# Softmax of attention tiles: exponentials head by head on ACT with a bias, in place of a subtraction and a sum on VectorE

## Chip, cores and metric

One core of one Trainium2 chip. The metric is the time of one execution in microseconds; the engines are named as in the profile: PE (TensorE matmul), PEld (its weight load), DVE (VectorE), ACT (ScalarE), POOL (GpSimd), SP (SyncE, which issues most DMAs).

## What is computed

Three layers in a row, all fp32: attention within chunks of 64 positions (8 batches, 8 heads, 576 positions, head size 64), a gated two-matrix layer (512 to 2048 to 512) on all 4608 tokens, and a layer of eight experts (512 to 1024 to 512) of which each token takes the best one, if its skip score is positive.

```python
scores = scale * np.matmul(q_c, k_c.transpose(0, 1, 2, 4, 3))
scores = scores - np.max(scores, axis=-1, keepdims=True)
attn = np.exp(scores)
attn = attn / (np.sum(attn, axis=-1, keepdims=True) + 1e-09)
out = np.matmul(attn, v_c)
...
h = x @ w_in
g = h * (1.0 / (1.0 + np.exp(-1.702 * h)))
return (g @ w_out).astype(np.float32)
```

## The kernel before, in words

The attention works on 36 tiles of 128 positions, all 8 heads of a tile at once. A tile goes through these steps (class `Att`): `a` transposes q and k on PE (line 141) and copies them out of PSUM on ACT (143); `b_mm` makes the scores with 32 small matmuls of 64x64 into two PSUM banks, one for even and one for odd heads (158); `b_post` is the softmax up to the exponential (160 to 173); `c0` on DVE sums, adds 1e-9, takes the reciprocal and multiplies (175 to 182); `c1` transposes the probabilities on PE (187) and copies them out on ACT (189); `d_mm` multiplies with v, again in 64x64 matmuls (207), and `d_post` copies the result out into `x1` (212). On PE one 64x64 matmul of the program stands as two records in the trace.

Four tiles come first, before any of the second layer can start. While they run, and during the first block behind them, the second layer's weights are converted from 64-bit floats, in 32 halves: ACT (`r`, 255; `lf`, 256), DVE (262, 263), POOL (264), ACT (`whi`, 276), DVE (`wlo`, 277). The function `tick` sets how they are interleaved.

The second layer then runs over nine blocks of 512 tokens. A block starts with `split_x1`, which splits its input into two parts, `xh` on ACT (285) and `xl` on DVE (286), and has 16 rounds. A round is 12 matmuls 128x512 into `hps` (`emit_h`, 296), a `tanh` on ACT (299), a product on DVE (300), a cast on ACT (`gh`, 306), a difference on DVE (`gl`, 307) and 12 matmuls into `yps` (`emit_y`, 316 to 320). The other 32 attention tiles are spread over the first eight blocks, five in the first and four or fewer in each of the others. In the round of a `burst` PE makes the value matmuls of the tile before and the scores of the next one into the same two banks (`sv`); the two banks of that tag (`at`) also take the transposes and the small routing matmuls. DVE does the gates of the third layer (353) between. The experts' layer follows behind the ninth block.

The engines each work through their queue in order. What order that is, a scheduler decides when the program is built: it plays the program's instructions through a model and places each where it finds it ready. The source therefore sets the dependencies and a preference, and a change of one engine's work can change the order of all engines.

## Time and profile before

| | us |
|---|---|
| median of 3 runs | 1224.9 (1224.62 to 1226.09) |
| the profiled execution | 1227.84 |
| its span in the trace | 1226.1 |
| PE busy | 1182.7 (96%) |
| DVE busy | 783.9 (64%) |
| ACT busy | 490.2 (40%) |
| POOL busy | 144.6 (12%) |

The span is the time from the first to the last record. Busy time is the sum of the time in which an engine had an instruction running; PE's matmuls are pipelined, so a busy PE need not be at its peak. The rows further down say which line, engine and tile they belong to; "L173" is line 173 of the kernel.

### The profile page before, as it was taken

What the parts mean: (1) busy time and instruction counts of PE and PEld (TensorE: products, weight loads), DVE (VectorE), ACT (ScalarE), POOL (GpSimd) and SP (SyncE); (2) the same over time, 40 slices, a digit from 0 to 9 for tenths busy, and PEclk for the clock granted to TensorE, in tenths of its full rate; (3) what the DMA queues carried; (4) which work ended last, traced back from release to release, by engine and by line L of the source; (5) the groups of instructions that cost most, each with busy time, mean ns of one, the idle gap of its engine ahead of it and who ended that gap; (6) DMA issues with size and microseconds to landing.
All of it is one profiled execution on the core that took longest, in us unless ns stands there. A gap on an engine that the chain in (4) does not pass through costs nothing. (4 is left out here: it accounts for less than half of the span.)

```text
span 1226.1 us, 20893 instructions
## 1 busy us (share of the span) xinstructions
PE 1182.7 (96%) x7984; PEld 991.8 (81%) x7984; DVE 783.9 (64%) x1771; ACT 490.2 (40%) x825; POOL 144.6 (12%) x137
## 2 busy tenths in 40 slices
PE   6798999999999999999999999999999999999995
PEld 4576788888888888888888888888788989999885
DVE  5889578369349548647736935943985686665531
ACT  5867443343332333324334333332344454444320
POOL 2344000010010010000001001001021023231110
PEclk9999999999999999999999999999999999999998
DMA  9756331131122113113113113202344677666540
GB/s 211 208 175 178 112 102 27 44 104 26 27 68 78 28 31 107 32 31 95 35 36 104 26 28 92 55 10 69 130 139 131 215 170 265 215 228 227 195 144 8
DMA packets 181848, 129.00 MB, mean 105 GB/s; under 512 B 122336, under 2 KB 155360, under 8 KB 181617
## 3 DMA queue, kind: packets, MB, share of 16 engines
q1 hardware_dynamic: 177072, 117.09, 33.4%
q0 software_dynamic: 4672, 10.54, 2.5%
q8 instruction: 64, 1.05, 0.4%
q14 instruction: 40, 0.32, 0.1%
HBM read 103.59 MB, written 25.04 MB: 105 GB/s over the span
## 5 line engine op out<-in xcount | busy, mean ns | idle before, releaser
L316 PE MATMUL yps<-whi,gh 128*128 128x512 f32 x576 | 228.7, 397 | 6.4 <-ACT gh L306 6.4
L296 PE MATMUL hps<-xh,whi 128*128 128x512 f32 x576 | 231.6, 405 | 3.2 <-DVE sg L300 3.2
L296 PE MATMUL hps<-xl,whi 128*128 128x512 f32 x576 | 227.5, 395 | 0.0
L296 PE MATMUL hps<-xh,wlo 128*128 128x512 f32 x576 | 227.0, 394 | 0.0
L317 PE MATMUL yps<-wlo,gh 128*128 128x512 f32 x576 | 225.6, 392 | 0.0
L300 DVE SCALAR_TENSOR_TENSOR sg<-sg,hps 128x512 f32<-128x512 f32 x144 | 98.3, 684 | 172.1 <-ACT sg L299 171.1
L353 DVE CUSTOM_DVE_ANT_0 junk<-x,wg 128x512 f32<-128x512 f32 x256 | 175.8, 687 | 4.0
L543 DVE TENSOR_TENSOR elo<-rawe,ehi 128x1024 fp32r<-128x1024 f32 x88 | 107.6, 1224 | 84.6 <-ACT ehi L542 84.5
L320 PE MATMUL yps<-whi,gl 128*128 128x512 f32 x576 | 156.0, 393 | 0.0
L299 ACT ACTIVATE sg<-hps 128x512 f32<-128x512 f32 x144 | 85.8, 598 | 163.4 <-PE hps L296 163.2
L542 ACT CAST ehi<-rawe 128x1024 fp32r<-128x1024 f32 x88 | 92.3, 1049 | 139.6 <-PE h2p L608 69.4
L306 ACT ACTIVATE gh<-sg 128x512 fp32r<-128x512 f32 x144 | 91.0, 632 | 118.3 <-DVE sg L300 104.8
L316 PEld LDWEIGHTS yps<-whi,gh 128*128 128x128 f32 x576 | 108.3, 188 | 30.9 <-ACT gh L306 7.8
L296 PEld LDWEIGHTS hps<-xh,whi 128*128 128x128 f32 x576 | 108.5, 190 | 26.3 <-DVE sg L300 4.1
L296 PEld LDWEIGHTS hps<-xh,wlo 128*128 128x128 f32 x576 | 108.9, 189 | 22.6
L320 PEld LDWEIGHTS yps<-whi,gl 128*128 128x128 f32 x576 | 108.0, 189 | 22.6 <-DVE gl L307 0.3
L317 PEld LDWEIGHTS yps<-wlo,gh 128*128 128x128 f32 x576 | 108.5, 188 | 21.8
L296 PEld LDWEIGHTS hps<-xl,whi 128*128 128x128 f32 x576 | 109.2, 190 | 20.6
L307 DVE SCALAR_TENSOR_TENSOR gl<-sg,gh 128x512 fp32r<-128x512 f32 x144 | 99.0, 688 | 33.4 <-ACT gh L306 21.7
L406 POOL DMA_INDIRECT tab<-pr,pos x36 | 37.8, 1049 | 682.3 <-DVE st L166 335.0
L608 PE MATMUL h2p<-xT,ehi 128*128 128x256 f32 x640 | 117.2, 283 | 0.0
L608 PEld LDWEIGHTS h2p<-xT,ehi 128*128 128x128 f32 x640 | 101.9, 191 | 2.6
(172 smaller groups left out, 1520.5 us busy)
## 6 DMA issues: line engine op xcount, KB each, us to landing
rawe<-in_moe_w_dram SPq DMA_DIRECT2D x88, 512.0 KB, 4.0
v<-in_v_dram SPq DMA_DIRECT2D x144, 64.0 KB, 2.7
x2d<-x SPq DMA_DIRECT2D x36, 256.0 KB, 3.1
out_dram<-x SPq DMA_DIRECT2D x36, 256.0 KB, 3.8
q<-in_q_dram SPq DMA_DIRECT2D x32, 256.0 KB, 3.7
k<-in_k_dram SPq DMA_DIRECT2D x32, 256.0 KB, 3.7
raw<-in_moe_w_in_dram SPq DMA_DIRECT2D x16, 512.0 KB, 4.0
raw<-in_moe_w_out_dram SPq DMA_DIRECT2D x16, 512.0 KB, 3.3
```

The source lines that it names most:

```text
L296: PE.matmul(ps, a, b[:, kk], start=(n == 0), stop=(n == 3 * KD - 1))
L299: ACT.activation(out=sg, in_=ps, func=AF.Tanh, scale=0.851)
L300: DVE.scalar_tensor_tensor(sg, sg, 1.0, ps, op0=ALU.add, op1=ALU.mult)
L306: ACT.activation(out=gh, in_=sg, func=AF.Copy, scale=0.5)
L307: DVE.scalar_tensor_tensor(gl, sg, 0.5, gh.bitcast(F32), op0=ALU.mult, op1=ALU.subtract)
L316: PE.matmul(ys[t], gh[:, cs], wh, start=first, stop=False)
L317: PE.matmul(ys[t], gh[:, cs], wl, start=False, stop=False)
L320: PE.matmul(ys[t], gl[:, cs], wh, start=False, stop=last)
L353: DVE.tensor_tensor_reduce(junk, xs[t], wg[:, e, :] if e < NE else ws, 1.0, 0.0, ALU.mult, ALU.add, lg[:, t, e:e + 1])
L542: ACT.copy(out=hi, in_=raw)
L543: DVE.tensor_tensor(lo, raw, hi.bitcast(F32), op=ALU.subtract)
L608: PE.matmul(ps[:, f], a[:, c], self.xT[:, b, kk], start=(m == 0), stop=(m == 3 * KD - 1))
```

## The change

The maxima go into a tile `nm`, which is multiplied by minus the softmax scale. ACT then makes the exponentials of each of the eight heads by itself, 64 numbers a row, straight from the scores in PSUM, with the head's negative scaled maximum as bias, and adds up each head's sum into `st`. The two subtractions, the exponential over all heads and the sum on DVE are gone. From here on the changed kernel's lines are one less than before's (ACT's `tanh` is L298 in place of L299, the value matmuls L206 in place of L207).

```diff
         def b_post(self, ps):
 
             self.p = self.T[0].rearrange("p j (g k) -> p j g k", g=2)
-            pw = self.p.rearrange("p (x h) g k -> p h g x k", h=2)
             self.st = ap.tile([P, NHP, 2], F32, tag="st", name="st", bufs=2)
+            sc = float(D) ** -0.5
+            nm = ap.tile([P, 2, NHP], F32, tag="nm", name="nm", bufs=2)
             for h2 in range(2):
-                DVE.tensor_reduce(self.st[:, :, h2], ps[h2], axis=AX.X, op=ALU.max)
-            for h2 in range(2):
-                DVE.tensor_tensor(
-                    pw[:, h2], ps[h2].rearrange("p (g x) k -> p g x k", g=2),
-                    self.st[:, :, h2:h2 + 1].rearrange("p (g x) o -> p g x o", g=2).to_broadcast(
-                        [P, 2, 2, CH]), op=ALU.subtract,
-                )
-            ACT.activation(out=self.p, in_=self.p, func=AF.Exp, scale=float(D) ** -0.5)
+                DVE.tensor_reduce(nm[:, h2], ps[h2], axis=AX.X, op=ALU.max)
+            DVE.tensor_scalar(nm, nm, -sc, None, op0=ALU.mult)
+            for hp in range(NHP):
+                for h2 in range(2):
+                    g, j = divmod(2 * hp + h2, NHP)
+                    ACT.activation(out=self.p[:, j, g], in_=ps[h2][:, hp], func=AF.Exp, scale=sc,
+                                   bias=nm[:, h2, hp:hp + 1], accum_out=self.st[:, j, g:g + 1])
 
         def c0(self):
-            DVE.tensor_reduce(self.st, self.p, axis=AX.X, op=ALU.add)
             DVE.tensor_scalar(self.st, self.st, 1e-9, None, op0=ALU.add)
             DVE.reciprocal(out=self.st, in_=self.st)
```

The scheduler places things anew, on all engines. Three places follow, of the kernel before and of the changed one apart; the tiles are the out and in of a row, and "x4" counts equal neighbours.

On DVE, the start of the program, from the maxima of the first tile on. Before:

```order
L166 TENSOR_REDUCE st<-s_170 128x4
L166 TENSOR_REDUCE st<-s_171 128x4
L168 TENSOR_TENSOR bA<-s_170,st 128x2x2x64
L168 TENSOR_TENSOR bA<-s_171,st 128x2x2x64
L262 TENSOR_SCALAR r<-r 128x512
L263 SCALAR_TENSOR_TENSOR a<-raw_110,r 128x512
L176 TENSOR_REDUCE st<-bA 128x8
```

Now:

```order
L167 TENSOR_REDUCE nm<-s_170 128x4
L167 TENSOR_REDUCE nm<-s_171 128x4
L168 TENSOR_SCALAR nm<-nm 128x8
L176 TENSOR_SCALAR st<-st 128x8
L177 RECIPROCAL st<-st 128x8
L178 TENSOR_TENSOR bA<-bA,st 128x512
L261 TENSOR_SCALAR r<-r 128x512
L262 SCALAR_TENSOR_TENSOR a<-raw_110,r 128x512
```

The first weight conversion (`r`, `a`) stood ahead of the first tile's sum and normalization, and now stands behind the normalization, which needs all eight exponentials.

On ACT, a burst in the middle of the program, from the `tanh` ahead of it on. Before:

```order
L299 ACTIVATE sg<-hps 128x512
L306 ACTIVATE gh<-sg 128x512
L212 COPY x_3691<-sv_4241 128x2x128
L173 ACTIVATE qT<-qT 128x512
L212 COPY x_3692<-sv_4242 128x2x128
L299 ACTIVATE sg<-hps 128x512
```

Now:

```order
L298 ACTIVATE sg<-hps 128x512
L305 ACTIVATE gh<-sg 128x512
L172 ACTIVATE qT,st<-sv_4877,nm 128x64
L172 ACTIVATE qT,st<-sv_4878,nm 128x64
L172 ACTIVATE qT,st<-sv_4877,nm 128x64
L172 ACTIVATE qT,st<-sv_4878,nm 128x64
L172 ACTIVATE qT,st<-sv_4877,nm 128x64
L172 ACTIVATE qT,st<-sv_4878,nm 128x64
L172 ACTIVATE qT,st<-sv_4877,nm 128x64
L172 ACTIVATE qT,st<-sv_4878,nm 128x64
L211 COPY x_4786<-sv_4877 128x2x128
L211 COPY x_4787<-sv_4878 128x2x128
```

One row between the two copies became eight rows ahead of both; the next `tanh` stands behind them.

On PE, the 64x64 matmuls of a burst (line 206 or 207: values; 158: scores) in the same stage. Before, a whole burst ends:

```order
L158 MATMUL sv_4751<-kT,qT 64x64
L158 MATMUL sv_4752<-kT,qT 64x64
L158 MATMUL sv_4751<-kT,qT 64x64
L158 MATMUL sv_4752<-kT,qT 64x64
L296 MATMUL hps<-xh,whi 128x512
L296 MATMUL hps<-xl,whi 128x512
```

Now, in one burst, the change from values to scores:

```order
L206 MATMUL sv_4877<-qT,v 64x64
L206 MATMUL sv_4878<-qT,v 64x64
L158 MATMUL sv_4877<-kT,qT 64x64
L315 MATMUL yps<-whi,gh 128x512
L316 MATMUL yps<-wlo,gh 128x512
L319 MATMUL yps<-whi,gl 128x512
L158 MATMUL sv_4878<-kT,qT 64x64
L158 MATMUL sv_4877<-kT,qT 64x64
```

And in another, the first value matmul alone:

```order
L295 MATMUL hps<-xl,whi 128x512
L295 MATMUL hps<-xh,wlo 128x512
L206 MATMUL sv_5350<-qT,v 64x64
L315 MATMUL yps<-whi,gh 128x512
L316 MATMUL yps<-wlo,gh 128x512
```

The 16 value and 16 score matmuls of a burst stood in one stretch in most bursts; in the changed kernel large matmuls stand between them in some bursts.

## Rows read from the trace of the kernel before

**Rows 1.** The page's first part: busy us (share of the span) and instructions.
```profile
PE 1182.7 (96%) x7984; PEld 991.8 (81%) x7984; DVE 783.9 (64%) x1771; ACT 490.2 (40%) x825; POOL 144.6 (12%) x137
```

**Rows 2.** Stages: start:end, length, busy us of PE, PEld, DVE, ACT, POOL; PEclk; DMA.
```profile
0.00:48.70 48.70, 29.92 (x352) 23.71 (x353) 30.96 (x66) 29.59 (x56) 13.21 (x22) 1.00 0.94 219
48.70:153.00 104.30, 95.97 (x649) 75.45 (x648) 85.79 (x135) 68.70 (x125) 37.13 (x24) 0.98 0.53 157
153.00:850.00 697.00, 697.00 (x4828) 573.38 (x4827) 440.17 (x1176) 241.19 (x445) 29.46 (x34) 1.00 0.20 53
...
9.59:47.25 37.66, 25.16 (x305) 19.89 (x306) 27.79 (x57) 25.69 (x50) 11.37 (x8) 1.00 1.02 239
60.00:120.00 60.00, 53.61 (x344) 41.64 (x343) 55.30 (x83) 43.37 (x78) 29.70 (x19) 0.97 0.60 176
...
80.00:100.00 20.00, 19.46 (x116) 15.12 (x115) 19.56 (x33) 15.78 (x29) 9.66 (x7) 0.92 0.71 197
```

**Rows 3.** What PE waited for, 48.7 to 153 us: us, times, longest.
```profile
PE yps L316 <- ACT gh L306: 6.4, 5, 3.0
PE hps L296 <- DVE sg L300: 1.4, 1, 1.4
```

**Rows 4.** Timeline of PE around 79 us: start, us, line, out<-in, count [idle before].
```profile
78.88 0.50 PE L316 MATMUL yps<-whi,gh 128*128 128x512 f32 x1 [2.99 <-ACT gh L306]
...
79.92 0.63 PE L316 MATMUL yps<-whi,gh 128*128 128x512 f32 x1
...
81.62 1.86 PE L320 MATMUL yps<-whi,gl 128*128 128x512 f32 x4
```

**Rows 5.** Groups by line: xcount | busy us, mean ns | idle us before.
```profile
L168 DVE TENSOR_TENSOR qT<-sv,st 128x256 f32<-128x256 f32 x64 | 23.8, 413 | 0.0
...
L176 DVE TENSOR_REDUCE st<-qT 128x8 f32<-128x512 f32 x32 | 21.8, 683 | 11.7 <-ACT qT L173 11.7
...
L177 DVE TENSOR_SCALAR st<-st 128x8 f32<-128x8 f32 x36 | 6.0, 167 | 0.7
...
L173 ACT ACTIVATE qT<-qT 128x512 f32<-128x512 f32 x32 | 20.2, 633 | 0.0
...
L370 ACT ACTIVATE ex<-dl 128x32 f32<-128x32 f32 x9 | 2.1, 229 | 8.9 <-DVE dl L369 8.9
...
L353 DVE DVE_READ_ACCUMULATOR2_ANT lg<- 128x1 f32 x288 | 23.4, 81 | 0.0
```

**Rows 6.** Timeline of ACT near 43 us; a single such copy takes 0.36 us.
```profile
43.31 0.64 ACT L212 COPY x<-pv 128x256 f32<-128x256 f32 x2
...
47.00 0.36 ACT L212 COPY x<-pv 128x256 f32<-128x256 f32 x1
```

**Rows 7.** Timeline of PE around three stretches of 64x64 matmuls.
```profile
465.48 0.39 PE L296 MATMUL hps<-xh,wlo 128*128 128x512 f32 x1
465.79 0.69 PE L207 MATMUL sv<-qT,v 64*64 64x64 f32 x32
466.31 0.65 PE L158 MATMUL sv<-kT,qT 64*64 64x64 f32 x32
...
467.22 0.39 PE L296 MATMUL hps<-xl,whi 128*128 128x512 f32 x1
...
835.71 0.39 PE L296 MATMUL hps<-xh,wlo 128*128 128x512 f32 x1
836.03 0.32 PE L207 MATMUL sv<-qT,v 64*64 64x64 f32 x2
...
836.62 0.39 PE L317 MATMUL yps<-wlo,gh 128*128 128x512 f32 x1
...
838.23 1.07 PE L320 MATMUL yps<-whi,gl 128*128 128x512 f32 x4
839.23 0.69 PE L207 MATMUL sv<-qT,v 64*64 64x64 f32 x30
...
840.19 0.39 PE L296 MATMUL hps<-xl,whi 128*128 128x512 f32 x1
```

## The prediction

> **What bounds the kernel now.** I read the busy shares first, then the stages, then PE's waits, then single rows. The page gives PE 96% of the span, DVE 64%, ACT 40% [rows 1]; that is an average over stages with different limits, so it cannot say what 36 softmaxes are worth. The stages can [rows 2]. Up to 48.7 us (four attention tiles, before the first expert-layer matmul) no engine is full: PE 29.9, DVE 31.0, ACT 29.6 of 48.7 us. From there to 153 us (the first of nine blocks, which also converts the 64-bit weights) PE is busy 96.0 of 104.3 us. From 153 to 850 us, where 27 of the 36 tiles get their softmax, PE is busy 697.00 of 697.00 us and the view of its waits is empty. DVE has 440 us of work there and ACT 241. So time taken off DVE in that stage is worth nothing, and time put on ACT costs nothing as long as PE still finds its operands ready; only what changes PE's own sequence counts. In the first block PE waits 6.4 us for `gh` and 1.4 us for `sg`, in pieces up to 3.0 us [rows 3]. One of these costs twice: after the gap that ends at 78.88 us the matmuls from 79.92 us on start 0.43 us apart instead of 0.227, and the window around them shows a granted clock of 0.92 (the 1.2 GHz level for a while, 2.4 GHz elsewhere). Eight matmuls lose about 8 x 0.2 = 1.7 us [rows 4]. So 9.5 us of that block are not PE work.
>
> **The change, part by part.** DVE loses per tile two subtractions (413 ns each) and one sum (683 ns) and gains a scaling of 8 numbers a row, for which the nearest row is the 167 ns addition of the same shape [rows 5]: -1.34 us a tile, -48 us in 36. In the stage from 153 us on this buys nothing, as said. In the stretch from 60 to 120 us DVE is busy 55.3 of 60 us and ACT 43.4 [rows 2], so there it can shorten what PE waits for.
>
> ACT loses one 512-wide exponential (633 ns) and gains eight 64-wide ones with their sums. No such row exists. The exponential over 32 takes 229 ns and over 512 633 ns [rows 5], so 64 alone take 229 + 32 x 404/480 = 256 ns. Two copies of 0.36 us fit into 0.64 us [rows 6], so neighbours overlap by 0.08 us: the lower bound is 0.17 us a piece, if the pointer to the bias and the sum cost nothing. Fetching the sum may be an operation of its own, as on DVE, where it takes 81 ns [rows 5]; the upper bound is one more instruction of ACT's shortest kind and no overlap, 256 + 229 = 485 ns. I take 0.35 us, near the middle of 0.17 and 0.49: 0.256 - 0.08, plus twice the 81 ns for sum and pointer. Eight take 2.8 us, +2.2 us a tile (0.7 to 3.3), +78 us in 36. The Trainium skill, "ScalarE: Activation LUTs", section "What ACT_TABLE_LOAD costs", gives 280 ns + 0.833 ns per element with a pointer bias and 93 ns of overlap between neighbours; by that a piece takes 0.24 us as an estimate, without the sum, and the total below would come out near 1231 us. No row here shows a pointer bias.
>
> *Before the first expert matmul.* Four tiles put 4 x 2.2 = 8.7 us on ACT. Between 9.59 and 47.25 us ACT is idle 37.66 - 25.69 = 12.0 us [rows 2], but its queue is in order and each tile's chain runs through it: the order shows seven of the eight exponentials of tile 0 ahead of the weight conversions, and DVE's next conversion behind that tile's normalization, so DVE, POOL and the conversions wait. I count half, +4.4 us (0, if all fits into idle time, to 8.7). The first `hps` matmul moves from 48.7 to about 53 us. It is partly repaid: in the order twelve first conversion steps (`r`) stand before the first `xh` instead of nine, so later conversions start from further ahead.
>
> *The first block.* Five tiles: DVE 85.8 - 6.7 = 79.1, ACT 68.7 + 10.9 = 79.6 of 104.3 us [rows 2]; neither becomes the bound over the block. DVE's relief, the conversions done earlier and PE's new order (four `hps` groups stand before the first `yps`, where it was three) speak for shorter waits, ACT's longer queue ahead of `gh` against it. I take half of the 9.5 us back, -4.7 (bounds -9.5 and 0).
>
> *PE's order in the blocks.* This is the largest term, and the diff does not show it. The scheduler now cuts the attention matmuls of a burst into more pieces. Counted in the order, the 64x64 matmuls (scores and values, in one go or with others between) form 4 stretches per block in blocks 1 to 6 before and 7 now, 5 and 8 in block 7, 6 and 4 in block 0. In each group of four bursts one is cut in three and one in two. The number of stretches of transposes and routing matmuls hardly moves (13 per block in most blocks, before and after). What a stretch costs, three places show [rows 7]. A whole one, 64 records between the 128x512 matmuls at 465.48 and 467.22 us, takes 1.74 us where two undisturbed steps take 0.453: 1.29 us extra. One of 2 records, between 835.71 and 836.62 us: 0.91 - 0.453 = 0.46 us. One of 30 records, between the last of the four at 838.23 (838.91 us) and 840.19 us: 1.28 - 0.453 = 0.83 us. From 2 to 30 records that is 0.0133 us a record; what is left is 0.43 us per stretch whatever its length, and 0.43 + 64 x 0.0133 = 1.28 gives the whole one back. The same number of records in three more stretches is 1.29 us a block; 7 blocks x 3 x 0.43 = **+9.0 us**, where PE has no idle time to hide it. In block 0 two fewer: -0.9 us. Bounds: 0.35 and 0.46 us per stretch, +7.4 to +9.7 us. The Trainium skill, "TensorEngine Tiling (Array Packing)", section "Key Properties", says that a change of the tiling mode, not of the tile, drains TensorE; it gives no figure. By that rule the new cuts must cost something and changing from values to scores nothing, and the rows agree: 0.43 us once, also where both follow each other.
>
> *The burst itself.* Does PE now wait for the longer softmax? In three of four bursts the transposes of the probabilities stand 36 large matmuls behind the scores, 36 x 0.227 = 8.2 us, where before it was 12 us or more in those blocks except one burst in four. The chain takes: two maxima, taken as long as the subtractions, 0.8, scaling 0.17, eight exponentials 2.8, addition and reciprocal, both 8 numbers a row, 0.4, the product, over as much as the old sum, 0.68 [rows 5], and some 0.5 for the handoffs, my estimate: 5.4 us. It fits with 2.8 us to spare. What stands behind the exponentials in ACT's queue, the two copies of `x1` and the next `tanh`, moves back by 1 to 2 us, and in the rounds behind a burst the `yps` stand 24 matmuls (5.4 us) or more behind their `hps`. I cost this at nothing; the cover is that slack.
>
> Sum: +4.4 - 4.7 - 0.9 + 9.0 = +7.8 us on the profiled execution's 1227.8 us (span 1226.1, the rest around it untouched), which is 2.9 us above the median of the runs. On the median of 1224.9 that is **1233 us**. The last stage, from 850 us on, has no softmax and its order keeps its shape.
>
> **The rivals.** *ACT is dearer and the start pays.* At 0.49 us a piece a tile adds 3.3 us; half of 13 us in the start is +6.5, the first block gives nothing back: 6.5 - 0.9 + 9.0 = +14.6, 1239.5 us. For it: the missing row. Against: 12 us of idle ACT time and 35 us idle in the first block. *The start gains, on the other side.* At 0.25 us or less the four tiles add at most 4 x 1.4 = 5.5 us, all within ACT's idle time, and DVE's relief takes away the whole 9.5 us of waits and slow clock: -9.5 - 0.9 + 9.0 = -1.4, 1223.5 us, not slower. For it: DVE busy 55.3 of 60 us. Against: every tile's chain gets longer. *The cuts are free*, because the array is drained anyway or the order is not what limits: 1233 - 9 = 1224 us. Against it stand three measured stretches. *The softmax comes late on PE.* Above 0.7 us a piece the chain passes 8.2 us; at 0.8 us it is 0.8 us late in some 21 bursts (+17), with +7 or more at the start: about 1258 us, and gaps could lower the clock as at 79.92 us.
>
> **How the numbers follow.** The forecast gets 0.63, dearer ACT 0.17, the gain at the start 0.09, free cuts 0.06, the late softmax 0.05. The range goes from 1226, the forecast with the lower price of a cut and nearly all waits gone, to 1243, dearer ACT with more than half of it unhidden; it leaves out the last three. Within 0.2% (2.4 us, about what a measurement tells from no change) lie half of the gain at the start, two thirds of the free cuts and 0.02 of the forecast: 0.11. Faster by more: 0.06. Slower: 0.83.
>
> **What would show it.** Right: in a block from 153 us on, `xh` recurs 1.3 us later than before, PE still without a wait, and lone 64x64 stretches cost 0.4 us each; ACT shows 288 exponentials of 0.25 to 0.5 us; the first `hps` starts at 51 to 57 us. Wrong: blocks of unchanged length, PE waiting for `pTp` or `gh` after 160 us, or the first block ending earlier than 153 us by more than 5 us.

## The result, and the profile after

The changed kernel takes 1242.9 us (median of 4 runs, 1240.95 to 1243.17); before took 1224.76 us beside it (4 runs). The ratio is 1.0143, with a 95% interval of 1.0126 to 1.0161: 18.1 us slower where 8.1 were forecast. Run again on another chip (e12 below) it took 1242.2 us beside 1227.02, ratio 1.0128 (1.0112 to 1.0144), 15.2 us slower. The direction held and the time lies just inside the range, which ended at 1243 us; the size was off by a factor of two.

The page's first part of the changed kernel answers to [rows 1]:

```profile
PE 1187.7 (96%) x7984; PEld 991.3 (80%) x7984; DVE 749.7 (60%) x1699; ACT 548.8 (44%) x1365; POOL 140.5 (11%) x137
```

DVE lost 34 us of work, ACT gained 59, and PE is as full as before. The stages of the changed kernel, cut where [rows 2] cut them (start:end, length, then busy us of PE, PEld, DVE, ACT, POOL, the granted clock, the DMA share and GB/s):

```profile
0.00:48.70 48.70, 25.17 (x328) 20.14 (x328) 25.95 (x53) 34.09 (x110) 12.53 (x21) 0.77 0.92 218
48.70:153.00 104.30, 94.38 (x594) 75.67 (x595) 82.50 (x127) 76.47 (x189) 34.13 (x24) 0.91 0.46 135
153.00:850.00 697.00, 696.03 (x4826) 565.69 (x4825) 411.61 (x1119) 283.29 (x858) 29.57 (x33) 1.00 0.21 56
```

In the last of them PE is again busy for all but 1 us, as in the kernel before, and yet the stage now ends later. A busy share cannot show that; the length of a block can. The next table takes the start of the first `xh` cast on ACT in each block, read from ACT's timeline, and splits the span by it. "Block 0" runs from the first such cast to that of the next block, "blocks 1 to 7" to that of the last block, "rest" from there to the end. All in us, from each kernel's profiled execution.

| kernel | first `xh` | block 0 | blocks 1 to 7 | rest | span |
|---|---|---|---|---|---|
| before | 47.25 | 109.54 | 692.11 | 377.20 | 1226.1 |
| changed | 52.93 | 109.79 | 698.94 | 377.54 | 1239.2 |
| changed, again (e12) | 53.56 | 109.86 | 696.81 | 380.17 | 1240.4 |

So the two profiles of the changed kernel lose 5.7 and 6.3 us before the first block, 0.3 in block 0, 6.8 and 4.7 in blocks 1 to 7, and 0.3 and 3.0 behind them: 13.1 and 14.3 us. The medians beside the first profile differ by more, 18.1 us, because the profiled execution of before was 3.1 us above the median of the runs beside it and the first one of the changed kernel 2.0 us below; where in the program those 5 us lie, no profile shows.

These marks are on ACT, and where they fall in PE's work moves with the order. Between the first two marks PE starts 364 of its 128x512 matmuls before and 371 now, between the second and the third 381 and 373. At 0.227 us each, block 0 looks 1.6 us too long by that, and block 1 1.8 us too short. The same spans cut at PE's own first `hps` matmul of each block, between which the work on PE is the same:

| kernel | first `hps` | block 0 | blocks 1 to 7 | rest |
|---|---|---|---|---|
| before | 48.73 | 110.82 | 691.32 | 375.25 |
| changed | 53.60 | 110.40 | 699.62 | 375.60 |
| changed, again (e12) | 54.23 | 110.47 | 697.49 | 378.19 |

By PE's marks the two profiles lose 4.9 and 5.5 us in the start, gain 0.4 and 0.3 in block 0, lose 8.3 and 6.2 in blocks 1 to 7 (2.1 of the 8.3 are two pauses, told of in the last section) and 0.3 and 2.9 behind.

**The start.** PE's scores and transposes of probabilities in the four first tiles, the timeline of before:

```profile
21.37 1.23 PE L158 MATMUL s<-bB,bA 64*64 64x64 f32 x32 [1.78 <-ACT bB L143]
...
36.44 1.09 PE L187 MATMUL pTp<-ident,bA 128*128 128x128 f32 x4 [0.21 <-ACT r L255]
```

and of the changed kernel:

```profile
24.00 1.13 PE L158 MATMUL s<-bB,bA 64*64 64x64 f32 x32 [1.02 <-ACT bB L143]
...
31.19 1.61 PE L158 MATMUL s<-bB,bA 64*64 64x64 f32 x32 [1.90 <-ACT bA L172]
...
41.66 1.06 PE L186 MATMUL pTp<-ident,bA 128*128 128x128 f32 x4
```

The third tile's scores come 2.6 us later than before, the last tile's probabilities 5.2 us, the first `xh` 5.7 us: the delay grows from tile to tile. What PE waited for up to 54 us shows where (us in total, times, longest; the two largest, for q from DMA, 7.9 us, and for ACT's copy `bB`, 4.3, are left out: before they were 7.2 and 3.6):

```profile
...
PE pv L206 <- ACT x L211: 3.7, 1, 3.7
PE qTp L141 <- ACT bA L172: 2.9, 1, 2.9
PE hps L295 <- ACT xh L284: 2.8, 1, 2.8
PE pv L206 <- ACT bA L188: 1.9, 2, 1.0
PE s L158 <- ACT bA L172: 1.9, 1, 1.9
```

All five end with ACT, two of them with the new exponentials (L172), which read the scores' banks that the next transposes and scores need. The order has a part in it from the first tile on. Behind the first of its eight exponentials stands the copy of the next tile's `qTp`, for which ACT idles although the other seven could run:

```profile
11.46 0.59 ACT L143 COPY bA<-qTp 128x512 f32<-128x512 f32 x1 [1.41 <-PE qTp L141]
```

That burst took 4.46 us from its first start to its last end, and the second tile's scores, behind it, start at 15.20 us in place of 14.15.

**What a softmax costs on ACT.** Two groups of the changed kernel, streamed tiles only, and behind them the first pieces of one burst of exponentials in ACT's timeline:

```profile
L172 ACT ACTIVATE qT<-sv,nm 128x64 f32<-128x64 f32 x256 | 76.3, 323 | 110.0 <-DVE nm L168 110.0
L172 ACT ACTIVATION_READ_ACCUMULATOR qT<-sv,nm 128x1 f32 x256 | 55.4, 217 | 0.0
```

```profile
37.68 0.30 ACT L172 ACTIVATE bA<-s,nm 128x64 f32<-128x64 f32 x1
37.88 0.20 ACT L172 ACTIVATION_READ_ACCUMULATOR bA<-s,nm 128x1 f32 x1
37.97 0.31 ACT L172 ACTIVATE bA<-s,nm 128x64 f32<-128x64 f32 x1
...
39.70 0.35 ACT L172 ACTIVATE bA<-s,nm 128x64 f32<-128x64 f32 x1
39.90 0.24 ACT L172 ACTIVATION_READ_ACCUMULATOR bA<-s,nm 128x1 f32 x1
```

The sum is fetched by an instruction of its own, of 217 ns on its mean, but the pairs follow each other 0.29 us apart ((39.70 - 37.68) / 7), so eight take 2.46 us from the first start to the last end; 34 of the 36 bursts take 2.45 to 2.53 us, the first two, with other work of ACT between, 4.46 and 2.96. The means of the two groups (540 ns together) would have given 4.3.

**A block.** PE's timeline of the changed kernel in one burst that the scheduler cut in three:

```profile
574.37 0.39 PE L295 MATMUL hps<-xh,wlo 128*128 128x512 f32 x1
574.69 0.56 PE L206 MATMUL sv<-qT,v 64*64 64x64 f32 x18
575.18 0.50 PE L315 MATMUL yps<-whi,gh 128*128 128x512 f32 x1
575.51 0.39 PE L316 MATMUL yps<-wlo,gh 128*128 128x512 f32 x1
...
576.67 0.84 PE L319 MATMUL yps<-whi,gl 128*128 128x512 f32 x3
577.45 0.40 PE L206 MATMUL sv<-qT,v 64*64 64x64 f32 x11
...
578.17 0.39 PE L316 MATMUL yps<-wlo,gh 128*128 128x512 f32 x1
578.41 0.40 PE L319 MATMUL yps<-whi,gl 128*128 128x512 f32 x1
578.73 0.69 PE L158 MATMUL sv<-kT,qT 64*64 64x64 f32 x30
579.35 0.50 PE L295 MATMUL hps<-xh,whi 128*128 128x512 f32 x1
579.69 0.39 PE L295 MATMUL hps<-xl,whi 128*128 128x512 f32 x1
```

By the prediction's own measure (from the large matmul ahead to the second one behind, less two undisturbed steps of 0.453 us) the three pieces cost 0.69, 0.60 and 0.83 us (the second counted from the last of the three `gl` matmuls, at 577.12), 2.12 us where a whole one costs 1.29 [rows 7]: 0.41 us a cut. A lone stretch of two records, which each block now has as well, costs 0.46 like its twin in [rows 7]. So the price that was forecast is there. What was missed stands in the kernel before, once in each of blocks 1 to 6 (block 1 has a second, milder one):

```profile
640.49 1.16 PE L320 MATMUL yps<-whi,gl 128*128 128x512 f32 x4
641.59 0.68 PE L207 MATMUL sv<-qT,v 64*64 64x64 f32 x16
642.10 0.22 PE L158 MATMUL sv<-kT,qT 64*64 64x64 f32 x1
...
642.28 0.51 PE L207 MATMUL sv<-qT,v 64*64 64x64 f32 x11
642.62 0.63 PE L158 MATMUL sv<-kT,qT 64*64 64x64 f32 x26
643.18 0.50 PE L296 MATMUL hps<-xh,whi 128*128 128x512 f32 x1
643.52 0.39 PE L296 MATMUL hps<-xl,whi 128*128 128x512 f32 x1
```

This burst is in one piece, but value and score matmuls alternate in it. From the last of the four `gl` matmuls (640.49 + 1.16 - 0.39 = 641.26) to 643.52 it takes 2.26 us, 1.81 us extra where a whole one in order costs 1.29. The changed kernel has none that costs this: its bursts change at most three times between values and scores, and a whole one that does so still costs 1.29 us (from 527.64 us on). Two cuts, a lone stretch and one alternation less are 0.83 + 0.46 - 0.52 = +0.77 us a block; blocks 2 to 6 are 0.80 longer (99.85 for 99.05, where no pause falls into one). Over blocks 1 to 7, the extra time of all these stretches, each measured in this way, is 39.6 us before and 45.7 in e12, which had no pause: 6.1 us, all but 0.1 of what those blocks are longer by PE's marks.

### The profile page after: what moved, and what is told of

It is laid out like the page before. It is cut to its first block, busy times and chain, and to the rows that moved or that the text cites. A ratio compares the mean times of both kernels' runs of the same rounds, so it can differ in the third digit from the quotient of the medians.

```text
span 1239.2 us, 21368 instructions
## 1 busy us (share of the span) xinstructions
PE 1187.7 (96%) x7984; PEld 991.3 (80%) x7984; DVE 749.7 (60%) x1699; ACT 548.8 (44%) x1365; POOL 140.5 (11%) x137
## 3 DMA queue, kind: packets, MB, share of 16 engines
q8 instruction: 64, 1.05, 0.4%
## 5 line engine op out<-in xcount | busy, mean ns | idle before, releaser
L299 DVE SCALAR_TENSOR_TENSOR sg<-sg,hps 128x512 f32<-128x512 f32 x144 | 98.4, 684 | 168.0 <-ACT sg L298 167.9
L298 ACT ACTIVATE sg<-hps 128x512 f32<-128x512 f32 x144 | 87.9, 612 | 188.9 <-PE hps L295 186.9
L542 DVE TENSOR_TENSOR elo<-rawe,ehi 128x1024 fp32r<-128x1024 f32 x88 | 107.5, 1223 | 85.7 <-ACT ehi L541 81.3
L172 ACT ACTIVATE qT<-sv,nm 128x64 f32<-128x64 f32 x256 | 76.3, 323 | 110.0 <-DVE nm L168 110.0
```

The costliest lines, as they stand in the source:

```text
L298: ACT.activation(out=sg, in_=ps, func=AF.Tanh, scale=0.851)
L299: DVE.scalar_tensor_tensor(sg, sg, 1.0, ps, op0=ALU.add, op1=ALU.mult)
L542: DVE.tensor_tensor(lo, raw, hi.bitcast(F32), op=ALU.subtract)
```

## The experiments

Theory 1: two separate costs, the start (its four tiles) and PE's order in blocks 1 to 7, while the longer softmax of the streamed tiles costs nothing by its own work. Rivals: the streamed softmax itself is on the path; all of it is the start and its slow clock. The runs' profiles, by the `xh` marks of the first table above:

| run | first `xh` | block 0 | blocks 1 to 7 | rest | ratio to before (95%) |
|---|---|---|---|---|---|
| e1 old start | 47.11 | 110.13 | 699.10 | 379.76 | 1.0102 (1.0084, 1.0121) |
| e2 old stream | 53.28 | 109.84 | 692.28 | 377.30 | 1.0049 (1.0032, 1.0066) |
| e3 new, values held | 53.09 | 109.80 | 687.97 | 378.74 | 1.0043 (1.0026, 1.0060) |
| e4 sums on DVE | 54.12 | 107.09 | 697.01 | 375.38 | 1.0086 (1.0068, 1.0103) |
| e5 old start, values held | 46.56 | 110.96 | 686.83 | 379.75 | 0.9990 (0.9978, 1.0003) |
| e6 more ACT work | 50.58 | 114.48 | 692.32 | 375.22 | 1.0061 (1.0047, 1.0076) |
| e7 before, no model | 46.52 | 121.89 | 688.91 | 375.18 | 1.0053 (1.0038, 1.0067) |
| e8 new, no model | 47.60 | 122.36 | 690.45 | 372.79 | 1.0073 (1.0059, 1.0088) |
| e9 before, PE held | 46.27 | 109.66 | 693.40 | 381.37 | 1.0044 (1.0030, 1.0059) |
| e10 new stream, PE held | 47.53 | 111.00 | 693.63 | 382.24 | 1.0058 (1.0044, 1.0073) |
| e11 third softmax, PE held | 50.49 | 109.58 | 693.13 | 381.80 | 1.0075 (1.0059, 1.0091) |
| e13 no sum | 43.89 | 109.22 | 692.12 | | |
| e14 banks held | 44.11 | 109.14 | 692.32 | 374.73 | 0.9990 (0.9979, 1.0000) |
| e15 e5, early lists | 46.72 | 110.20 | 686.94 | 384.04 | 1.0016 (1.0006, 1.0027) |
| e16 before, early lists | 45.93 | 109.61 | 692.11 | 381.85 | 1.0060 (1.0043, 1.0077) |
| e17 e14 with e5 | 44.02 | 115.11 | 688.17 | 380.10 | 1.0031 (1.0020, 1.0041) |
| e18 new, start held | 59.97 | 116.81 | 687.10 | 379.32 | 1.0162 (1.0147, 1.0178) |

**Splitting the change by tiles (e1, e2).** Both kernels carry both softmaxes and choose by the tile's number:

```diff
+        def new(self):
+            return self.t >= TPB        # e2: self.t < TPB
+        def b_post(self, ps):
+            (self.b_post_new if self.new() else self.b_post_old)(ps)
```

> Old softmax in the four tiles before the first expert matmul, new one in the 32 streamed tiles; PE's order in blocks 1 to 7 is the changed kernel's (7 stretches of 64x64 matmuls a block). Theory 1 (two separate costs: the start, and PE's order in the blocks): the first hps is back near 48.7 us, blocks 1 to 7 stay 6 to 7 us longer in all than before, the whole 1229 to 1234 us. Rival (the long softmax of the streamed tiles makes all of it): 1240 to 1243 us. Rival (all of it is the start and its slow clock): 1224 to 1227 us.

> The reverse: new softmax in the first four tiles only, old one in all streamed tiles; PE's order in blocks 1 to 7 is that of the kernel before. Theory 1: the first hps at 53 to 54 us as in the changed kernel, with a stretch of half clock before it, blocks 1 to 7 of 99.05 us as before; 1230 to 1237 us. Rival (streamed tiles make all of it): 1224 to 1227 us.

Measured 1238.67 us (+11.6) and 1233.49 (+6.4) beside 1227.07. The halves add up to the whole: 18.0 us (18.1 and 15.2 measured). e2 has PE's order of before in blocks 1 to 8, row for row, and its blocks' length; all of its loss lies ahead of the first `xh`. e1 has the changed kernel's order in blocks 1 to 7, and blocks that are 7.0 us longer, 2.2 of them two pauses at the places where the first profile has them. Its total is above what was expected, by 5 us: 0.6 in block 0 and 2.6 in the rest were not foreseen. e1 is also a test of block 0 by itself: the start is the old one (47.11 for 47.25 us), the block has the new softmax in its own five tiles and PE's new order, and it is 0.6 us longer (110.13), by PE's marks 0.1 shorter (110.73).

**Order against work in the blocks (e3, e9, e10, e11, e7, e8).** e3 is the changed kernel with one edge more in each streamed burst:

```diff
         def d_mm(self, ps):
+            first = self.t >= TPB
...
-                            PE.matmul(ps[g][o, x, cc], self.v[r, c, j, :], self.pT[r, j, cc],
-                                      start=True, stop=True)
+                            mm = PE.matmul(ps[g][o, x, cc], self.v[r, c, j, :], self.pT[r, j, cc],
+                                           start=True, stop=True)
+                            if first:
+                                tc.keep_in_program_order(mm)
+                                first = False
```

> The changed kernel, with the first value matmul of each streamed burst held behind the PE instructions that stand ahead of it in the program: the 64x64 matmuls form 4 whole stretches a block again (7 in the changed kernel, 4 with one that alternates in the kernel before), and 10 stretches of transposes instead of 13. The softmax, its engines and its work are the changed kernel's. Theory 1 (cuts cost 0.4 us each): blocks 1 to 7 are 1.3 to 1.8 us shorter than in the changed kernel, 98.0 to 98.6 us each, the whole 1231 to 1234 us. Rival (the longer softmax is what lengthens the blocks, the cuts are free): blocks stay at 99.8 us, or PE waits for pTp or gh, 1241 to 1245 us.

Blocks 2 to 6 of 98.29 us (one of 99.04, with a pause), 8.8 us less in blocks 1 to 7 than in e12, 687.97 for 696.81, with the same softmax on the same engines: 1232.04 us. PE's order is what lengthened the blocks, and the cuts above all: a block of e3 pays 5.20 us extra for its four whole bursts, one of the changed kernel 6.47 for its seven pieces, 1.27 of the 1.56 us that its blocks are shorter. The edge also took three of 14 stretches of transposes and routing matmuls out of a block.

e9 to e11 give PE one and the same order from block 1 on, by holding every matmul and transpose behind the one ahead of it in the program (the transposes by the same line):

```diff
+        def matmul(*a, **k):
+            mm = nc.tensor.matmul(*a, **k)
+            return tc.keep_in_program_order(mm) if PE.held else mm
...
     for j in range(NB):
+        PE.held = 1 <= j < NB
```

e9 does it to the kernel before, e10 to e1's mixture. e11 has a softmax that stands between the two: one maximum per row and bank as the bias, so that two exponentials of 256 columns do, and the sum on DVE:

```diff
+            nm = ap.tile([P, 2], F32, tag="nm", name="nm", bufs=2)
+            for h2 in range(2):
+                DVE.tensor_reduce(nm[:, h2:h2 + 1], ps[h2].rearrange("p h k -> p (h k)"), axis=AX.X, op=ALU.max)
+            DVE.tensor_scalar(nm, nm, -sc, None, op0=ALU.mult)
+            for h2 in range(2):
+                ACT.activation(out=pw[:, h2], in_=ps[h2].rearrange("p (g x) k -> p g x k", g=2), func=AF.Exp,
+                               scale=sc, bias=nm[:, h2:h2 + 1])
```

> The kernel before, with all of PE's matmuls and transposes from block 1 on held in program order (start and block 0 as the scheduler has them): 4 whole stretches of 64x64 matmuls a block where one alternated before, 8 of transposes instead of 13. Theory 1 (a block pays for its stretches): blocks 1 to 6 of 98.2 to 98.7 us instead of 99.05, the whole 2 to 5 us shorter than before. Rival (the order is worth nothing, or held matmuls wait): blocks of 99.0 us or more, the whole not below before.

> Old softmax in the first four tiles, new one in the streamed tiles, PE from block 1 on held in program order: the order of PE in blocks 1 to 7 is that of the run before this one. Theory 1 (the new softmax lengthens blocks 1 to 7 by the order alone): blocks within 0.25 us of the run before this one. Rival (its own work lengthens them): 0.8 us or more a block.

> A third softmax, in all 36 tiles: one maximum per row over the four heads of a PSUM bank as the bias, so two exponentials of 256 columns from PSUM instead of eight of 64, the sum on VectorE as before, no subtraction; PE held in program order from block 1 on. VectorE loses two subtractions a tile, ScalarE gains one instruction's fixed time, some 0.2 us, instead of 1.7. Theory 1 (the start and block 0 follow ScalarE's queue, blocks 1 to 7 PE's order): the first hps within 1.5 us of 48.7, blocks as in the two runs before, the whole 1220 to 1225 us, 2 to 6 us under before. Rival (anything on the start's chain that is not ScalarE's queue, such as the bias, is what costs): hps at 52 us or later, the whole over 1226 us.

One block of each, from one first `xh` cast to the next (columns as in the stages above), e9, e10 and e11:

```profile
453.94:553.25 99.31, 98.89 (x694) 81.25 (x693) 63.44 (x166) 34.14 (x64) 4.04 (x5) 1.00 0.21 54
```

```profile
456.69:556.04 99.35, 98.93 (x694) 81.23 (x693) 59.16 (x158) 40.94 (x125) 3.90 (x5) 1.00 0.21 54
```

```profile
457.95:557.24 99.29, 98.87 (x694) 81.23 (x693) 61.87 (x162) 34.59 (x68) 4.03 (x5) 1.00 0.21 54
```

This is the cleanest reading of the study on the streamed softmax: with PE's order fixed, four new softmaxes put 6.8 us more on ACT (1.7 a tile) and take 4.3 off DVE, and the block stays what it was, 99.31 against 99.35 us. The work is hidden whole. The expectation of e9 itself failed: the held order is no gain (99.32 us a block, where 98.2 to 98.7 was expected), since PE now waits 0.4 us a block for `gh` and for a PSUM bank; and in the last block, which was held too, routing matmuls wait 4.4 us for a maximum on DVE. That makes the rest 4 to 5 us longer in all three, so their totals say nothing on the softmax. e11's start went against its expectation: ACT has 0.1 us a tile more to do than before there, and yet the first `xh` came 3.2 us later than before (50.49) and the whole took 1236.64 us. ACT's work can hardly be the reason there; the scheduler's order of the start is another again.

e7 and e8 leave the order to the scheduler without its model of times (one switch; the expectations call it program order, though in the start the rows do not follow the program line for line). PE's rows agree between the two from block 1 to the end.

```diff
-    with _tile.TileContext(nc, schedule_with_timeline_sim=True) as tc:
+    with _tile.TileContext(nc, schedule_with_timeline_sim=False) as tc:
```

> The kernel before with the instructions in the order of the program, not the scheduler's: 4 whole stretches of 64x64 matmuls in each of blocks 1 to 6, 9 of transposes. To be read against the next run, which has the same order of PE with the new softmax. The start may be slower than the scheduled one by several us. Theory 1: blocks 1 to 7 of about 98.2 us if the order leaves PE no wait.

> The changed kernel in program order: PE's order in blocks 1 to 7 is the same as in the run before this one, so only the softmax differs. Theory 1 (in the blocks the change acts through the order alone): blocks 1 to 7 within 0.2 us a block of the run before this one, the whole longer only by what the start costs, 3 to 8 us. Rival (the longer softmax delays PE in the blocks by itself): blocks longer by 0.5 us or more each, with waits for pTp or gh, the whole over 9 us longer.

1232.98 and 1234.76 us: under this order the whole change costs 1.8 us, not 15 to 18. The blocks are 98.64 and 98.87 us, 0.23 apart where the expectation allowed 0.2, which makes 1.5 us in blocks 1 to 7, most of the 1.8. The list of waits is empty in both; in block 4 the difference stands at one place, where two steps into `yps` take 0.33 and 0.34 us for 0.23. So in this order the longer softmax is not quite free. The first `xh` moves by 1.1 us only. Most of the loss therefore hangs on orders that the scheduler makes with its model.

**The start (e4, e6, e13, e14, e18).** e4 takes `accum_out` off the exponentials and puts the sum back on DVE; e6 and e14 put work on ACT in the kernel before, behind the exponential of the first four tiles; e13 leaves DVE's sum out in the first nine tiles. The edits of e4, of e6 and e14, and of e13:

```diff
-                               bias=nm[:, h2, hp:hp + 1], accum_out=self.st[:, j, g:g + 1])
+                               bias=nm[:, h2, hp:hp + 1])
         def c0(self):
+            DVE.tensor_reduce(self.st, self.p, axis=AX.X, op=ALU.add)
```

```diff
+            if self.t < TPB:                                  # e6; e14: 2 of them, in_=ps[h2][:, 0]
...
+                for n in range(2 * NHP):
+                    tc.keep_in_program_order(ACT.activation(
+                        out=jk, in_=self.T[1][:, n % NHP, 0:CH], func=AF.Exp, scale=float(D) ** -0.5))
```

```diff
         def c0(self):
-            DVE.tensor_reduce(self.st, self.p, axis=AX.X, op=ALU.add)
+            if self.t >= TPB + 5:
+                DVE.tensor_reduce(self.st, self.p, axis=AX.X, op=ALU.add)
```

> The changed kernel without the sums on ScalarE: the eight exponentials keep their bias and lose their sum, and VectorE sums the probabilities as before (683 ns a tile). PE's order in blocks 2 to 6 has 6 stretches and the alternating one. Theory 1: without the 288 separate reads of the sum a burst of eight exponentials takes 1.5 to 2 us instead of 2.33, and the first hps comes 1 to 3 us earlier than in the changed kernel (53.6); the blocks stay within 0.3 us of 99.8 each; the whole 1238 to 1242 us. Rival (the count of reads is the cost): 1230 to 1235 us. Rival (VectorE's sum is on the path of the start again): later than 53.6, over 1243 us.

> The kernel before, and behind each of the first four tiles' exponentials eight exponentials of 64 columns more on ScalarE, from kT into a scratch tile that nobody reads; nothing waits for their results, so only ScalarE's queue is longer, by about 8 x 0.25 = 2 us a tile. Theory 1a (the start pays because ScalarE's queue is longer): the first hps 3 to 6 us later than 48.7 us, the whole 3 to 7 us longer than before. Rival 1b (the start pays because the chain maximum, scale, exponentials, product is longer; ScalarE's idle time takes extra work): hps within 1.5 us of 48.7, the whole within 2 us of before.

In e4 eight exponentials without a sum take 1.75 us (ACT's timeline of e4, duration of the eight):

```profile
36.18 1.75 ACT L172 ACTIVATE bA<-s,nm 128x64 f32<-128x64 f32 x8
```

That is 0.71 us less than with sums, 0.09 per fetched sum. The first `xh` came no earlier for it (54.12), against the expectation; block 0 became 2.7 us shorter (1.3 by PE's marks: 109.11 for 110.40), the blocks 697.0 as expected, the total 1236.71, a little under what was expected. e6, with no change to the chain of any tile, cost 7.3 us, as much as the real softmax in the start (e2: 6.4): the first `xh` 3.3 us later and block 0 4.9 us longer (the first `hps` 2.5 us later, less than the 3 to 6 expected and more than rival 1b's 1.5). With the order that the scheduler made for it, work that only lengthens ACT's queue was paid for in the start and in block 0; rival 1b falls.

> The kernel before without VectorE's sum of the probabilities in the first nine tiles (four at the start, five in block 0), so that these tiles' probabilities are divided by what stands in the tile in its place: 9 x 0.68 = 6.1 us less on VectorE there, ScalarE's work untouched. The prediction's step (VectorE's relief takes away waits of the first block): block 1 begins 2 to 5 us earlier than at 156.8 us, the whole 2 to 5 us shorter than before. Rival (the first block follows ScalarE's queue and the conversions; VectorE's relief buys nothing): block 1 begins within 1 us of 156.8, the whole within 1.5 us of before.

> The kernel before, and behind each of the first four exponentials two small ones on ScalarE that read the two PSUM banks of the scores into a scratch tile: the banks come free only when ScalarE has passed them, as with the new softmax, while ScalarE gets just 2 x 0.25 us a tile more. Theory 2 (the start also pays because the scores' banks are held until ScalarE's exponentials): first hps 2 us or more later than 48.7, the whole 2 to 5 us over before. Rival (only the length of ScalarE's queue counts): a quarter of what eight small exponentials cost, hps within 1 us of 48.7, the whole within 2 us of before.

e13 sends tokens to other experts, so only its trace up to the last block can be read. Block 1 begins at 153.1 us, 3.7 us earlier, as the prediction's step would have it. But 3.4 of these lie ahead of the first `xh`; block 0 itself took 109.22 us for 109.54 (109.66 for 110.82 by PE's marks), and PE's waits in it rose from 8.2 to 10.2 us. And in e14, where DVE does all its work and ACT 0.4 us a tile more, block 1 begins at 153.3. e14 also speaks against theory 2: banks held by ACT cost nothing there. Both gains come with a new order in the start, and e13 cannot show that DVE's relief made its own. e14's total is 0.999 of before's, not a difference that can be told.

> The new softmax in all tiles; PE, ScalarE and VectorE held in the order of the program up to the first xl, the streamed bursts' first value matmuls held as well. Theory 3 (most of the 5 to 6 us by which the start is later belongs to the order that the scheduler makes for it, not to the work): the first hps at 47 to 51 us, where the scheduled start with the same work gives 53.6 to 54.9. Rival (the work itself costs it): hps at 52 us or later.

```diff
...
+            return lambda *a, **k: tc.keep_in_program_order(f(*a, **k))
...
+    held[0] = True
     for tau in range(TPB + 3):
...
     xh, xl = split_x1(x1)
+    held[0] = False
```

e18 holds PE, ACT and DVE in the program's order through the start, with the new softmax: the first `hps` comes at 60.6 us, block 1 at 176.8, and the whole takes 1244.68 us. Theory 3's number failed; this order is worse than the scheduler's (PE waits 12.3 us for DVE's product), so it does not price the work by itself either.

**The same kernel again, and a faster version (e12, e5, e15, e16, e17).**

> The changed kernel once more, for a second profile. Theory 1: the first hps at 53 to 55 us, block 0 of 109 to 111 us, blocks 1 to 7 of 698 to 700 us in all as in the first profile, whatever clock the start is granted; the whole 15 to 20 us longer than before. Rival (the slow clock that the first profile shows from 23 to 60 us is part of the cost): where the start has full clock, the first hps comes 2 us or more earlier.

Blocks 1 to 7 took 696.8 us, a little under the range given, because this execution has no pause of the kind that the first profile shows twice. The first `xh` is no earlier although the granted clock reads 1.00 from 20 to 46 us, where the first profile has 0.50 from 23 to 43. The rival falls.

> Old softmax in the first four tiles, new one in the streamed tiles, and the first value matmul of each streamed burst held in program order (4 whole stretches of 64x64 matmuls a block). Theory 1 (the start and PE's order are the two costs, the streamed softmax itself costs nothing): the first hps at 47.8 to 48.8 us, blocks 2 to 7 of 98.3 us, 5 us less in all than before: 1220 to 1223 us where before takes 1225 to 1227. Rival (the streamed softmax costs something of its own beside the order): 1226 to 1232 us.

e5 (e1's mixture with e3's edge) has the shortest blocks, 5.3 us less in all than before, and 1225.84 us beside 1226.54; the 1220 to 1223 us expected were not reached. Block 0 takes back 1.4 us and the rest 2.6. The last wait on PE there is for the last expert's rows, behind a look-up of its list; e15 and e16 look the lists up two experts ahead:

```diff
-                if s + 1 >= NEARLY:
-                    if n == 0:
-                        slots[s + 1].list(first_row(s + 1))
-                    elif n == 1:
+                if n == 0 and NEARLY <= s + 2 < NS:
+                    slots[s + 2].list(first_row(s + 2))
+                if s + 1 >= NEARLY:
+                    if n == 1:
```

> Old softmax in the first four tiles, new one in the streamed tiles, the first value matmul of each burst held in program order, and in the last stage each expert's list is looked up two experts ahead instead of one, so that PE does not wait for the rows of the last expert: the two things that kept the version with the old start and the held values from being faster. Theory 1: blocks of 98.4 us, the last wait for xg (3.0 us there) gone or under 1 us, the whole 3 to 5 us under before (1222 to 1224 where before takes 1227). Rival (the wait is for the transfer of the rows, not for the list): the wait stays at 2 to 3 us, the whole within 1.5 us of before.

> The kernel before with the lists looked up two experts ahead, nothing else: tells what of the run before this one belongs to the lists. Theory 1: its wait for xg (1.3 us) goes, 1 to 2 us under before. Rival: no difference, within 1 us.

> The start of the run with the held banks (old softmax in the first four tiles with two small exponentials behind each, whose profile began block 1 at 153.3 us), and in the streamed tiles the new softmax with the first value matmul of each burst held in program order (blocks of 98.4 us). Theory 1 (start and blocks add up, each by its order): block 1 begins at 152 to 155 us, blocks 2 to 7 of 98.4 us, the whole 4 to 8 us under before, so faster than both kernels. Rival (the held banks' start was one lucky profile, or the last stage takes it back): within 2 us of before.

Early lists are a loss (e15 1227.77 us beside 1225.92, e16 1232.36): the wait for the rows stays (3.0 us in e15, 1.6 in e16), and a new one of 3.3 to 4.3 us for `hl` comes ahead of `y2p`. e17, e5 with the two small exponentials of e14, kept e14's early start (44.0 us), but block 0 took 115.1 us. No version was found that is faster than the kernel before by more than the measurement can tell.

## Why the prediction was wrong in size

- **"Blocks 1 to 7: 3 more 64x64 stretches per block x 0.43 = +9.0."** Right in kind and in price (0.41 to 0.46 us a cut), and e3 shows that it is the order that is paid for. Too large by 2.8 us: by PE's marks blocks 1 to 7 are 6.2 us longer in the profile without pauses, 1.0 in block 1, 0.80 in each of blocks 2 to 6 and 1.2 in block 7. The burst that alternates in the kernel before was counted as one stretch like the others and costs 0.5 us more than they do, in each of blocks 1 to 6. The Trainium skill's rule that a change of the tiling mode drains TensorE ("TensorEngine Tiling (Array Packing)", section "Key Properties") agrees with the cuts, 0.41 to 0.46 us each. The prediction drew from it that changing from values to scores costs nothing; that holds for one change and for three (1.29 us both times), not for the eleven of the burst that alternates (1.81).
- **"The first block: half of the 9.5 us back, -4.7", and -0.9 for two stretches.** This is the step that failed: block 0 is 0.3 us longer by the `xh` marks and 0.4 and 0.3 shorter by PE's, where -5.6 was forecast. The waits for `gh` [rows 3] did go, but others, for copies on ACT, took their place:

```profile
PE qTp L141 <- ACT x L211: 2.8, 1, 2.8
PE pTp L186 <- ACT qT L143: 1.7, 1, 1.7
PE hps L295 <- DVE sg L299: 1.4, 3, 0.8
PE hps L295 <- DVE xl L285: 0.3, 1, 0.3
```

  These are PE's waits in block 0 (its first `xh` wait, 2.8 us, belongs to the start): 6.2 us, and 7.6 in e12, where before had 8.2. And PE was slow for longer. Steps of 0.36 us or more between neighbouring large matmuls, with no wait and nothing between, number 16 before, 28 in the first profile and 22 in e12, and cost 3.3, 5.9 and 4.8 us over the usual 0.227. Waits and slow steps together are 11.5 us before, 12.0 and 12.4 now: nothing of them came back. By PE's marks the first profile adds up: -2.05 of waits, +2.58 of slow steps, -1.23 of the two stretches less (0.9 forecast) and +0.28 of small differences make -0.42. The prediction had counted the slow steps behind one wait alone; before has nine more at the head of the block, among them:

```profile
49.73 0.63 PE L296 MATMUL hps<-xl,whi 128*128 128x512 f32 x1
50.16 0.63 PE L296 MATMUL hps<-xh,wlo 128*128 128x512 f32 x1
```

  DVE was not idle for its relief: from 60 to 120 us it is busy 56.0 us (55.3 in [rows 2]), now with conversions that come later, as everything does behind a later start. Three runs bear on the term: the block's own change, with the old start, gave 0.1 us back (e1, by PE's marks); DVE's relief without any work put on ACT 1.2 (e13); and work moved back from ACT to DVE made the block shorter, not longer (e4). Each has an order of its own in the start or in this block, so that ACT's queue in place of DVE is what they point to, not what they prove.
- **"I count half, +4.4 us" for the start.** The work was overestimated and its cover too. A tile puts 1.7 us more on ACT, not 2.2: eight pieces took 2.46 us, not 2.8. But more of it was paid: by the mark that the prediction named, the first `hps`, the start lost 4.9 and 5.5 us of 4 x 1.7 = 6.8, not half. So the sum was near, 4.4, by two errors that cancel. e6 shows that a longer queue on ACT alone can cost this much. e8, e11, e14 and e18 show that the order of the start moves it by as much, in both directions; how much of the 5 us is the work and how much the order stays open.
- **"The burst itself … I cost this at nothing."** Right: e10 against e9, 0.04 us a block where PE's order is held; 0.2 in the order of e7 and e8.
- **"The rest around it untouched."** Not quite. In the profiles of the changed kernel, e1, e3 and e5 the rest is 377.5 to 380.2 us, in those of before, e2 and e6 375.2 to 377.3. A part of it is PE's wait for the last expert's rows, 2.2 to 3.2 us against 1.3 to 1.6. These kernels' order in the last block differs from before's only in some cases, and the cause was not found.
- **The price of one exponential.** 0.35 us was taken, 0.29 measured, 0.22 without the sum. The estimate from the Trainium skill, "ScalarE: Activation LUTs", section "What ACT_TABLE_LOAD costs", 0.24 us without the sum, was close.
- **The rivals.** "ACT is dearer and the start pays" came nearest (+14.6), for another reason than it gave: its 0.49 us a piece were not there, but the start did pay and the first block gave nothing back. "The start gains" fell with both. "The softmax comes late on PE" and "the cuts are free" are ruled out by e10 and e3.

Added up by PE's marks in the first profile: 4.9 - 0.4 + 8.3 + 0.3 = 13.1 us, where the prediction's terms were +4.4, -5.6, +9.0 and 0, in all 7.8. The largest error by far is block 0, and the 2.1 us of pauses hide most of the error in the blocks.

Of what was to be seen in the trace, the exponentials (323 ns), the first `hps` (53.6 and 54.2 us), the lone stretches (0.46 us) and a PE without waits in the blocks, but for the pauses, came true; `xh` recurs 0.8 us later per block, not 1.3.

## What to carry to other kernels

Where an engine has no idle time, look for what the change does to that engine's own order, and price every piece of that order, in the kernel before as well: an interruption that goes away is worth as much as one that comes. Take no credit for a wait that goes until the order behind it is read to the next wait: here each went, and another took its place. Cut the time at marks of the engine that bounds it, not of another, or work slips over the mark and looks like a gain here and a loss there. And where a scheduler places the instructions, a change of one instruction's duration can move the time by more than the duration: hold the order fixed in both kernels to see what the work costs.

## What the runs showed beside that

**The granted clock of the start did not show in PE's rows.** In the first profile of the changed kernel the granted clock reads 0.50 (the 1.2 GHz level) from 23 to 43 us, in e2, with the new softmax in the same four tiles, 1.00. The stretch from 30 to 40 us of the one and of the other (columns as above; the granted clock is the third number from the end), and the row of PE for the fourth tile's scores in e2:

```profile
30.00:40.00 10.00, 4.92 (x69) 4.10 (x70) 4.93 (x12) 8.18 (x36) 3.11 (x3) 0.50 0.82 217
```

```profile
30.00:40.00 10.00, 4.83 (x68) 4.00 (x68) 4.88 (x12) 8.03 (x35) 3.29 (x3) 1.00 0.84 209
```

```profile
31.36 1.61 PE L158 MATMUL s<-bB,bA 64*64 64x64 f32 x32 [1.89 <-ACT bA L196]
```

These 32 records take 1.61 us, as long as at 0.50 (the row at 31.19 us further up); in the blocks 32 of them take 0.65 [rows 7]. The slow steps at the head of block 0 before, 0.43 us apart, also stand where the granted clock reads 1.00. So in a stretch with many waits the granted clock alone does not tell PE's pace: read the steps of the rows. And two profiles that differ in it, as the two of the changed kernel do (first `xh` at 52.93 and 53.56 us), are no test of what a slow clock costs.

**A pause on PE.** In the first profile of the changed kernel two bursts took 1.05 us longer than their equals, without a wait that the profile can name. One of them in PE's timeline:

```profile
251.81 0.87 PE L158 MATMUL sv<-kT,qT 64*64 64x64 f32 x21
253.06 0.45 PE L158 MATMUL sv<-kT,qT 64*64 64x64 f32 x11 [0.38 <-issue]
```

The other is in the last burst of block 2, at the same record. e1 has both again, at the same places, e3 the one in block 1; the second profile of the changed kernel has none. So it depends on the execution whether they come, while the place comes again; the cause was not found. They make one profile's blocks 2 us longer than another's; a difference of that size in one profile is not yet the change's.
